# S4 convolution kernel: the low powers with their amplitude by exponentials and a product in PSUM, the first block's seeds ahead of its steps, its gate on the result

## The chip, the cores and the metric

The program runs on one core of a Trainium2 chip. Its time is the device time of one execution in microseconds (us), lower is better. The engines of the core are PE (TensorE: matmuls, with PEld for the loading of weights), DVE (VectorE), ACT (ScalarE), POOL (GpSimd) and SP (SyncE, which here issues most transfers). Each has an instruction queue of its own that runs in order, and they wait for each other by semaphores. SBUF and PSUM are the memories on the chip; PSUM takes the results of PE.

## The reference, cut to what matters

All arrays are float32; B = 1, L = S = 2048, D = 640, N = 192, F = 1536.

```python
def _A_ref(u, A_re, A_im, B_re, B_im, C_re, C_im, log_dt, Dskip):
    dt = jnp.exp(log_dt)[:, None]
    logdA = dt * (A_re + 1j * A_im)
    dB = dt * (B_re + 1j * B_im)
    l = jnp.arange(L)
    P = jnp.exp(logdA[:, :, None] * l[None, None, :])
    K = jnp.einsum("dn,dnl,dn->dl", C_re + 1j * C_im, P, dB).real
    # y = causal convolution of u with K along L, by FFTs of length 2 L
    ...
    return y + u * Dskip[None, None, :]

def _B_ref(x, w_gate, w_up, w_down):
    return ((x @ w_gate) * (x @ w_up)) @ w_down

x = A_u
sa, ca, ga, sb, cb, gb = the six rows of (_silu(c) @ w_mod)
h = _layernorm(x) * (1 + ca) + sa
x = x + ga * _A_ref(h, ...)
h = _layernorm(x) * (1 + cb) + sb
return x + gb * _B_ref(h, w_gate, w_up, w_down)
```

For one channel and one state, with rho and theta the real and imaginary parts of dt A, and amp and psi the size and the angle of C dB, the kernel K needs amp exp(rho l) cos(theta l + psi) for 2048 values of l, summed over the 192 states.

## The kernel before

**Tiling.** The 640 channels are taken in NB = 5 blocks of 128 (P). A block's 192 states are taken in 2 halves of 96, and a half in 4 steps of 24, so there are 40 steps (NK) of 24 states and 10 halves. The 2048 values of l are split into a low part (powers 0 to 7, times 64 for one of two tables) and a high part, so that a long table is an outer product of two short ones.

**The seeds of a block** (u_seeds) are made in segments, SEG0 for block 0 in the startup and SEG for the others in the loop, each letter a small step. s_l loads; s_a to s_c turn A, B and C into rho, theta and the product of B and C in a PSUM tile with the states transposed. s_d(h) makes the integer angles of half h by shifts (DL and DH, the low and the high ones). s_r(h) makes the multiples of rho: RL (1, 2 and 4 times rho) and RH (11 multiples for the high parts). s_e takes exponentials on ACT: seven powers of exp(64 rho) into LP, RH in place, RL in place. s_f, s_G, s_g and s_h give amp and the arctangent of the angle, transposed into PSUM; s_v copies amp into RL's fourth row and turns the angle into the integer psi. For block 0, s_e of the second half is put off (LATE, due at 15000).

**The tables** are POOL's. tab_ph(hf) makes LH, the low angles of half hf, with psi added in `weighted`. tab_eq(hf) makes LQ, amp times exp(rho l) for l = 0 to 7: one copy, one product and two doublings from RL. For each step n, `outer` (L817) writes three tables: Ph (LH plus DH, integer angles), EP (LP times RH) and EQ (LQ times RH). EP, EQ and the angle tables have two buffers each, LQ and LH one.

**A step** has four parts: ACT turns angles into sine and cosine by trig() (an Abs, a sine, and a cosine as the sine of pi/2 less the Abs) into PSUM tiles tra and trb, used in turn; DVE multiplies them with EQ and EP into QtA, PtA, PtB and QtB (L872, L878, L898); PE sums products over states into the PSUM tile kg (L913, L928). In trig(), where the source tile may be overwritten (the PtA parts), the Abs is taken in place of it; otherwise it goes to an SBUF tile `ab`.

**Around the steps** run, piece by piece, the FFT stages on PE (u_pre reads the normalized input h back, u_g, u_c and u_d go to the spectrum and back), the modulation rows from w_mod (L458), the statistics of the layer norm (u_stats: BN_STATS and BN_AGGR, L568) and the writing of x2d. In u_pre the four pieces of block 0 are multiplied by the gate row, on POOL (L966); for the other blocks the gate is in dt2 and dcol already. In u_d the result of the convolution in PSUM is added to the input, xs (L1110).

**What sets the order.** Table SCHED gives each piece a due time: a number of thousands for a half step of the loop, with 2t and 2t+1 for pass t of `for t in range(3 * NK + 24)`, and negative thousands for the startup, whose segments are SEG0's. Pieces are written out in the order of their due times; each engine then takes its own in that order. SP's queue holds the loads in that order too: a load into a buffer in use stands there until the buffer is free, and what is behind it stands as well. After the loop, from about 536 us on, comes the tail: the second layer norm and the GLU, in matmuls.

`act` (L320) is the helper through which every operation of ACT goes.

Of the kernel before, what the change touches and what calls it, by code (L numbers as in the profile page):

```python
# [10 lines left out]
F32 = mybir.dt.float32  # L11
# [21 lines left out]
    mr=(((-87997, 8001), (-87996, 11000)), ((-87999, 2000), (-88997, 8000)), ((-88999, -86998), (-89000, -87998))),  # L33
    st=(
        (-88993, 5000),
        (-101000, -92000),
# [4 lines left out]
        (-94000, -87995),  # L41
        (-98000, -87994),
        (1000, 20000),
        (1, 19000),
        (-91998, -87000),
        (-88995, 6000),
        (-87993, 13000),
        (-99000, -91000),
        (-88994, 16001),
        (-98998, -86999),  # L50
# [22 lines left out]
    e0=(15000,),  # L73
# [101 lines left out]
    low=(  # L175
        (14000, 40001, 64000, 88000, 111001, 139000, 163000, 187000, 209000),
        (18000, 42001, 68001, 92001, 113000, 139001, 163001, 185002, 209002),
    ),
# [136 lines left out]
def tile_kernel(ctx: ExitStack, tc: tile.TileContext, I, out):  # L315
# [20 lines left out]
    mults = const.tile([P, 14], F32, name="mults")  # L336
    for k, m in enumerate((1536, 1024, 512, 0, 8, 16, 24, 32, 40, 48, 56, 1, 2, 4)):
        V.memset(mults[:, k : k + 1], float(m))
# [60 lines left out]
    shr = kconst.tile([P, D], F32, name="shr")  # L399
    t_tw = kconst.tile([P, 32, 2, 64], F32, name="t_tw")  # L400
# [70 lines left out]
    def u_fold():  # L471
# [17 lines left out]
        V.tensor_tensor(sh[:, 0:1], sh[:, 0:1], gg[:, 0:1], op=OP.mult)  # L489
# [12 lines left out]
        act(xa[:, 4, 0:P], pt[:, P : 2 * P])  # L502
# [83 lines left out]
    LQ = pk1.tile([P, 96, 8], F32, name="LQ")  # L586
# [4 lines left out]
    RL = pk1.tile([P, 2, 4, 96], F32, name="RL")  # L591
    DH = [pk1.tile([P, 4, 192], I32, name=f"DH{i}") for i in range(3)]
    DL = [pk1.tile([P, 4, 192], I32, name=f"DL{i}") for i in range(2)]
    for d_ in DH:
        V.memset(d_[:, 0], 0)

    def u_seeds(db):
# [5 lines left out]
        prm = pk1.tile([P, 2, N], F32, name="prm")  # L603
        cr, ci = tb_[:, 2, :], tb_[:, 3, :]
        rho, f, amp = prm[:, 0, :], prm[:, 1, :], prm[:, 0, :]
        x, u, y, v = tb_[:, 0, :], tb_[:, 1, :], ta[:, 1, :], ta[:, 1, :]
# [24 lines left out]
        def free(h, *kinds):  # L631

            hf = 2 * db + h
            for k_ in kinds:
                if k_ in ("ph", "ep", "eq") and hf >= 3:
                    need(1, k_, 4 * (hf - 3) + 3)
                elif k_ in ("lh", "lq") and hf >= 2:
                    need(1, k_, hf - 2)
# [15 lines left out]
        def s_b():  # L654
            pb = bank("pb")
            act(pb, tb_[:, 0:2, :])
            V.tensor_tensor(ta, pb, cr.unsqueeze(1).to_broadcast([P, 2, N]), op=OP.mult)
            V.tensor_tensor(pb, pb, ci.unsqueeze(1).to_broadcast([P, 2, N]), op=OP.mult)
            V.tensor_tensor(x, ta[:, 0, :], pb[:, 1], op=OP.subtract)
            V.tensor_tensor(y, ta[:, 1, :], pb[:, 0], op=OP.add)  # L660
# [9 lines left out]

        def s_d(h):
            ps, q = T["ps"], T["q"]
            sti = q[:, 1].bitcast(I32).rearrange("p (s r) -> p s r", r=24)
            free(h, "lh", "ph")
            if h == 0:
                V.tensor_copy(sti, ps[:, 1])
# [6 lines left out]
            if h:  # L683
                V.tensor_tensor(t64, sti, shl[:, 5:6].unsqueeze(2).to_broadcast([P, 8, 24]), op=OP.logical_shift_left)
            mark("step", 2 * db + h)

        def s_r(h):
            ps = T["ps"]
            free(h, "ep", "eq", "lq")
            V.tensor_tensor(g4(Rl[h])[:, 0:3], ps[:, 0, hs[h]].unsqueeze(1).to_broadcast([P, 3, 4, 24]),  # L690
                            mults[:, 11:14].unsqueeze(2).unsqueeze(3).to_broadcast([P, 3, 4, 24]), op=OP.mult)
            V.tensor_tensor(g4(Rh[h]), ps[:, 0, hs[h]].unsqueeze(1).to_broadcast([P, 11, 4, 24]),
                            mults[:, 0:11].unsqueeze(2).unsqueeze(3).to_broadcast([P, 11, 4, 24]), op=OP.mult)
# [10 lines left out]
        def s_e(*hh):  # L704
            lp, rh, rl = (halves(R, hh) for R in (LP, RH, RL))
            for l in range(1, 8):
                act(lp[:, :, :, l], rl[:, :, 0], AF.Exp, scale=64.0 * l)
            act(rh, rh, AF.Exp)
            act(rl[:, :, 0:3], rl[:, :, 0:3], AF.Exp)
            for h in hh:  # L710
                mark("lp", 2 * db + h)

        def s_f():
# [3 lines left out]
            V.scalar_tensor_tensor(amp, u, dt2[:, db : db + 1], pe[:, 1], op0=OP.mult, op1=OP.mult)  # L717
            V.scalar_tensor_tensor(pe[:, 0], pe[:, 0], 1e-37, u, op0=OP.max, op1=OP.add)
            V.reciprocal(pe[:, 0], pe[:, 0])
# [4 lines left out]
        def s_G():  # L724
            if db:
                ps = bank("ps2")
            else:
                ps = ring(ps_tr, [P, 2, 512], "tr")[:, :, :N]
            T["ps2"] = ps.rearrange("p c (s r) -> p c s r", r=24)
            trans(amp, T["ps2"][:, 0])  # L730
            if db == 0:
                for h in range(2):
                    act(g4(Rl[h])[:, 3], T["ps2"][:, 0, hs[h]])
# [9 lines left out]
        def s_v():  # L743
            ps = T["ps2"]
            if db:
                for h in range(2):
                    V.tensor_copy(g4(Rl[h])[:, 3], ps[:, 0, hs[h]])
            V.tensor_scalar(psi, ps[:, 1], 4294967296.0 / math.pi, 536870912.0, op0=OP.mult, op1=OP.add)

            def weighted(h):  # L750
# [1027 lines left out]
```

## Time and profile before

| | us |
|---|---|
| runs of the kernel before | 990.01, 992.87, 998.23 |
| their median | 992.87 |
| the profiled execution | 990.33 |
| its span in the trace | 988.6 |
| PE busy | 887.3 (90%) |
| DVE busy | 760.7 (77%) |
| ACT busy | 579.9 (59%) |
| POOL busy | 577.4 (58%) |

The span is from the first to the last instruction of the trace; 1.7 us of the execution lie around it. The granted clock of TensorE was 0.958 of full speed over the span. "Busy" is the time in which an engine ran an instruction that does work. A row of a timeline gives the start, the duration of one instruction, the engine, the line, the operation and out<-in; in square brackets stands how long the engine had been idle before and what ended it. Rows of a chain of waits give the start, the time that the chain spends there, the engine and what it did. Rows of sums of waits read: engine, output and line, what it waited for, us in total, times, longest. The page's lines as they bear on the change stand in the prediction.

### The profile page before, as it was taken

What the parts mean: (1) busy time and instruction counts of PE and PEld (TensorE: products, weight loads), DVE (VectorE), ACT (ScalarE), POOL (GpSimd) and SP (SyncE); (2) the same over time, 40 slices, a digit from 0 to 9 for tenths busy, and PEclk for the clock granted to TensorE, in tenths of its full rate; (3) what the DMA queues carried; (4) which work ended last, traced back from release to release, by engine and by line L of the source; (5) the groups of instructions that cost most, each with busy time, mean ns of one, the idle gap of its engine ahead of it and who ended that gap; (6) DMA issues with size and microseconds to landing.
All of it is one profiled execution on the core that took longest, in us unless ns stands there. A gap on an engine that the chain in (4) does not pass through costs nothing.

```text
span 988.6 us, 26668 instructions
## 1 busy us (share of the span) xinstructions
PE 887.3 (90%) x11190; PEld 726.3 (73%) x11190; DVE 760.7 (77%) x1311; ACT 579.9 (59%) x1019; POOL 577.4 (58%) x424
## 2 busy tenths in 40 slices
PE   4854898999798699989988999999999999999998
PEld 3643656676575477677666888889998888889998
DVE  8798479887988977896899877787585977677452
ACT  5769999977888797974664322235464332224330
POOL 4987899799779989960145667641022454451000
PEclk9976899999989989999999999999999999999999
DMA  7665666443545553558733453445536222212241
GB/s 243 240 172 196 224 211 205 142 138 120 142 151 142 172 155 106 183 187 281 217 102 106 134 186 104 137 159 168 198 134 216 85 80 80 81 54 77 83 161 54
DMA packets 141961, 148.96 MB, mean 151 GB/s; under 512 B 8976, under 2 KB 120080, under 8 KB 140432
## 3 DMA queue, kind: packets, MB, share of 16 engines
q1 hardware_dynamic: 140688, 146.33, 46.9%
q8 instruction: 88, 1.44, 0.6%
q10 hardware_dynamic: 1152, 0.92, 0.3%
q14 instruction: 33, 0.27, 0.1%
HBM read 108.36 MB, written 38.86 MB: 149 GB/s over the span
## 4 chain that ended last, share of the span: by engine, by line
PE 58%; DVE 14%; ACT 13%; issue 6%; POOL 5%; DMA 2%; SPq 0%; DVEq 0%; ACTq 0%; POOLq 0%
PE pa L1196 26%; PE pa L1611 16%; ACT tra L320 2%; ACT trb L320 2%; PE psfb L995 2%; DVE QtA L872 2%; PE psfc L995 2%; PE psfb L1055 1%; PE kg L928 1%; POOL EQ L817 1%; PE psfa L1055 1%; PE kg L913 1%; PE psfc L1055 1%; PE psfb L950 1%; PE psfa L995 1%
## 5 line engine op out<-in xcount | busy, mean ns | idle before, releaser
L817 POOL TENSOR_TENSOR EQ<-LQ,RH 128x1536 f32<-128x1536 f32 x40 | 124.2, 3105 | 15.1 <-DVE QtB L872 14.9
L320 ACT ACTIVATE z<-pa 128x512 f32<-128x512 f32 x24 | 14.4, 599 | 167.1 <-PE pa L1196 120.5
L1160 DVE TENSOR_TENSOR wsgl<-wga,wsgh 128x640 fp32r<-128x640 f32 x72 | 68.1, 948 | 46.8 <-ACT wsgh L320 46.6
L320 ACT ACTIVATE wsgh<-wga 128x640 fp32r<-128x640 f32 x72 | 52.6, 732 | 72.0 <-PE pa L1611 48.6
L1560 POOL TENSOR_TENSOR z<-z,s 128x512 f32<-128x512 f32 x24 | 33.5, 1394 | 98.6 <-DVE s L1559 98.6
L1611 PE MATMUL pa<-wsgh,sh 128*128 128x384 f32 (+1 forms) x304 | 69.6, 310 | 0.0
L1611 PE MATMUL pa<-wsgh,sl 128*128 128x384 f32 (+1 forms) x304 | 69.2, 308 | 0.0
L1611 PE MATMUL pa<-wsgl,sh 128*128 128x384 f32 (+1 forms) x304 | 69.1, 309 | 0.0
L1172 POOL TENSOR_TENSOR tf<-wur,wgb 128x256 f32<-128x256 f32 x24 | 19.2, 801 | 80.7 <-DVE wtl L1160 54.7
L817 POOL TENSOR_TENSOR EP<-LP,RH 128x768 f32<-128x768 f32 x40 | 66.1, 1652 | 0.0
L817 POOL TENSOR_TENSOR Phb<-LH,DH 128x1536 int32<-128x1536 int32 x20 | 62.3, 3113 | 2.2 <-ACT tra L320 2.1
L817 POOL TENSOR_TENSOR Pha<-LH,DH 128x1536 int32<-128x1536 int32 (+1 forms) x21 | 62.4, 2972 | 1.8 <-ACT trb L320 1.4
L872 DVE TENSOR_TENSOR QtA<-tra,EQ 128x1024 f32<-128x1024 f32 x40 | 47.0, 1216 | 17.0 <-ACT tra L320 8.5
L1160 DVE TENSOR_TENSOR wtl<-tf,wth 128x256 fp32r<-128x256 f32 (+1 forms) x72 | 59.9, 858 | 0.0
L872 DVE TENSOR_TENSOR QtA<-trb,EQ 128x1024 f32<-128x1024 f32 x40 | 47.0, 1215 | 12.2 <-ACT trb L320 7.0
L928 PE MATMUL kg<-QtB,PtB 64*32 64x64 f32 x2560 | 47.0, 225 | 8.1 <-DVE QtB L872 8.0
L928 PEld LDWEIGHTS kg<-QtB,PtB 64*32 64x32 f32 x2560 | 40.3, 112 | 15.5 <-DVE QtB L872 9.0
L1558 DVE TENSOR_TENSOR s<-pa,s 128x512 f32<-128x512 f32 x24 | 16.6, 690 | 45.2 <-PE pa L1196 40.1
L1196 PE MATMUL pa<-sl,wth 128*128 128x512 f32 x144 | 45.2, 395 | 2.1 <-DVE sl L1160 2.1
L1611 PEld LDWEIGHTS pa<-wsgh,sl 128*128 128x128 f32 x304 | 46.6, 188 | 0.0
L1611 PEld LDWEIGHTS pa<-wsgh,sh 128*128 128x128 f32 x304 | 46.5, 188 | 0.0
L1611 PEld LDWEIGHTS pa<-wsgl,sh 128*128 128x128 f32 x304 | 46.5, 188 | 0.0
(602 smaller groups left out, 2926.9 us busy)
## 6 DMA issues: line engine op xcount, KB each, us to landing
wga<-wdg SPq DMA_DIRECT2D x24, 640.0 KB, 3.9
wga<-B_w_gate SPq DMA_DIRECT2D x12, 640.0 KB, 6.1
wgb<-B_w_gate SPq DMA_DIRECT2D x24, 320.0 KB, 3.4
wur<-B_w_up SPq DMA_DIRECT2D x24, 320.0 KB, 3.9
xb<-x2d SPq DMA_DIRECT2D x6, 1280.0 KB, 6.8
TVb<-WD SPq DMA_DIRECT2D x22, 256.0 KB, 3.4
t_tw<-w_mod SPq DMA_DIRECT2D x3, 1600.0 KB, 7.4
t_ti<-w_mod SPq DMA_DIRECT2D x3, 1600.0 KB, 7.5
```

Of the source, the lines that this page charges most:

```text
L320: return S.activation(o, i, f, **kw)
L817: G.tensor_tensor(o.rearrange("p x (h l) -> p x h l", l=8), lo.unsqueeze(2).to_broadcast([P, rows, nh, 8]), hi.rearrange("p h x -> p x h") ...
L872: return [lambda h=h: V.tensor_tensor(Qt[:, :, :, 32 * h : 32 * h + 32], tr[:, ::-1] if h else tr[:, :, :, ::-1], e[:, :, 32 * h : 32 * h ...
L928: PE.matmul(kg[j * 32 : j * 32 + 32, dd, :], PtB[lo : lo + 64, c, r, :], QtB[lo : lo + 64, c, r, :], start=False, stop=dd == 7 and c == 1, ...
L995: PE.matmul(r[c][par * 64 : par * 64 + 64, i, :], t_tw[:, k0 + k, c, :], src[:, k, :], start=True, stop=True, tile_position=(0, par * 64))
L1055: PE.matmul(r[par][:, i], w, v, start=c == 0, stop=c == 1, tile_position=(lo, 0))
L1160: V.tensor_tensor(lo, v, hi, op=OP.subtract)
L1172: G.tensor_tensor(t[:, 0:2], u[:, 0:2], g[:, 0:2], op=OP.subtract)
L1196: PE.matmul(ps, w[a][:, k], x[b][:, l], start=n == 0 and m == 0, stop=n == 2 and m == len(ks) - 1)
L1558: V.tensor_tensor(S67[i], ps, S6[i], op=OP.add)
L1560: G.tensor_tensor(ZT[i], ZT[i], S67[i], op=OP.add)
L1611: PE.matmul(ACC[tb][t][c], x[:, ts], w[:, cs], start=st, stop=f == NF - 1 and n == 2 and (c == 0 or t % 2 == 1))
```

## The change

It has six parts.

1. **Low powers.** tab_eq is gone from POOL. LQ has three halves as buffers. ACT takes exp(rho l) for l = 1 to 7 into LQ in s_e, as it does for LP, in place of the exponentials of RL; s_q copies amp from its PSUM tile to LQ's power 0 and multiplies the seven others by amp out of PSUM, on DVE. RL keeps only rho, so s_r copies 96 values a half in place of the product of 288.
2. **PSI.** In `weighted`, POOL did two operations for each of the two halves. Now `plus` adds psi over all states of the block and `minus` is done for each half (four operations for block 0, three for the others).
3. **The first block's seeds.** SEG0 is put in another order: both halves' exponentials, LQ products and shifts are in the startup, LATE is gone, and EP of step 1 and EQ of step 0 are made earlier on POOL. In table `st` the second numbers of the block's statistics move behind those pieces; two modulation rows (`mr`) have their second parts in the loop.
4. **The gate.** u_pre no longer multiplies by the gate row on POOL; u_d of block 0 multiplies the result in PSUM by the row (tile ggr) on DVE ahead of adding it to xs. The row of shifts `sh` is no longer multiplied by it.
5. **trig().** Where the Abs went to `ab`, it goes into the PSUM tile in which the cosine then replaces it.
6. **Tiles.** DH is one tile for all, prm is gone, and the temporary ones of the seeds share places.

The diff, cut to its core:

```diff
-    mr=(..., ((-88999, -86998), (-89000, -87998))),
+    mr=(..., ((-88999, 1100), (-89000, 100))),
     st=(
...
-        (-101000, -92000),
+        (-101000, -87500),
...
-        (-94000, -87995),
-        (-98000, -87994),
+        (-94000, -85900),
+        (-98000, -85800),
...
-    e0=(15000,),
...
-SEG0 = ("l", "a", "b", "c", "ud", "r", "x", "e", "f", "G", "g", "D", "h", "v", "R", "")
-SEG = ("l", "a", "b", "c", "ud", "D", "r", "R", "x", "E", "f", "g", "h", "v")
-P_PH, P_EP, P_MOD = 3, 6, 1
+SEG0 = ("l", "a", "b", "c", "iud", "r", "x", "e", "f", "Gg", "q", "R", "hv", "DX", "", "Q", "")
+SEG = ("l", "a", "b", "c", "iud", "D", "r", "R", "x", "E", "f", "g", "h", "v")
+P_PH, P_EP, P_EQ, P_PSI, P_MOD = 3, 6, 9, 12, 1
...
-    LQ = pk1.tile([P, 96, 8], F32, name="LQ")
+    LQ = pk1.tile([P, 3, 96, 8], F32, name="LQ")
...
-            V.tensor_tensor(g4(Rl[h])[:, 0:3], ps[:, 0, hs[h]].unsqueeze(1).to_broadcast([P, 3, 4, 24]),
-                            mults[:, 11:14].unsqueeze(2).unsqueeze(3).to_broadcast([P, 3, 4, 24]), op=OP.mult)
+            V.tensor_copy(Rl[h].rearrange("p (s r) -> p s r", r=24), rho_)
...
             for l in range(1, 8):
-                act(lp[:, :, :, l], rl[:, :, 0], AF.Exp, scale=64.0 * l)
+                act(lp[:, :, :, l], rl, AF.Exp, scale=64.0 * l)
             act(rh, rh, AF.Exp)
-            act(rl[:, :, 0:3], rl[:, :, 0:3], AF.Exp)
+            for l in range(1, 8):
+                act(lq[:, :, :, l], rl, AF.Exp, scale=float(l))
...
+        def s_q(*hh):
+            lq, a = halves(LQ, hh), T["amp"][:, hh[0] : hh[-1] + 1]
+            V.tensor_copy(lq[:, :, :, 0], a)
+            V.tensor_tensor(lq[:, :, :, 1:8], lq[:, :, :, 1:8], a.unsqueeze(3).to_broadcast([P, len(hh), 96, 7]), op=OP.mult)
...
+            def plus(w):
+                G.tensor_tensor(t64[:, w], t64[:, w], psi[:, w], op=OP.add)
+
+            def minus(h):
+                G.tensor_tensor(g5(Dl[h])[:, 0, :, 0, :], t64[:, hs[h]], g5(Dl[h])[:, 0, :, 1, :], op=OP.subtract)
...
-    def tab_eq(hf):
...
-        G.tensor_copy(LQ[:, :, 0:1], rl[:, 3].unsqueeze(2))
-        G.tensor_tensor(LQ[:, :, 1:2], rl[:, 3].unsqueeze(2), rl[:, 0].unsqueeze(2), op=OP.mult)
-        double(LQ, (rl[:, 1], rl[:, 2]), OP.mult)
...
         if ab is None:
-            ab = pk.tile([P, 512], F32, name="ab", bufs=1)
-            av = ab
+            ab = av = cv
...
-        if db == 0:
-            G.tensor_tensor(h, h, xa[:, 4, 0:P].unsqueeze(1).to_broadcast([P, 4, P]), op=OP.mult)
...
+        if db == 0:
+            V.tensor_tensor(ps, ps, ggr.unsqueeze(1).to_broadcast([P, 4, P]), op=OP.mult)
         V.tensor_tensor(xs, ps, xs, op=OP.add)
```

On the engines this stands as follows. The first place is DVE in the startup, from the last small step of the angle (ptb or pta from psfb) on; st and mv are the statistics, and f16a and gha are tiles of the input rows that they read. Before:

```order
L722 TENSOR_SCALAR pta<-psfb 128x192
L568 BN_STATS st_282<-f16a 128x6 x2
L569 BN_AGGR mv_95<-st_282 128x2
L568 BN_STATS st_290<-gha 128x6 x2
L569 BN_AGGR mv_95<-st_290 128x2
L677 CAST DL_159<-psfc 128x4x24
L680 TENSOR_TENSOR DL_159<-psfa,shl 128x12x24
L680 TENSOR_TENSOR DH_156<-psfa,shl 128x8x24
L680 TENSOR_TENSOR DL_159<-psfa,shl 128x12x24
L680 TENSOR_TENSOR DH_156<-psfa,shl 128x8x24
L684 TENSOR_TENSOR ptb<-psfa,shl 128x192
L748 TENSOR_SCALAR ptb<-tra 128x192
```

After:

```order
L712 COPY LQ<-tra 128x96
L713 TENSOR_TENSOR LQ<-LQ,tra 128x96x7
L687 COPY RL<-psfc 128x96
L688 TENSOR_TENSOR RH<-psfc,mults 128x1056
L745 TENSOR_SCALAR ptb<-tra 128x192
L675 TENSOR_TENSOR ptb<-psfa,shl 128x192
L676 CAST DL_155<-psfc 128x4x24
L679 TENSOR_TENSOR DL_155<-psfa,shl 128x12x24
L679 TENSOR_TENSOR DH<-psfa,shl 128x8x24
L679 TENSOR_TENSOR DL_155<-psfa,shl 128x12x24
L679 TENSOR_TENSOR DH<-psfa,shl 128x8x24
L564 BN_STATS st_371<-f16a 128x6 x2
```

The first statistics now stand behind the LQ product of the first half, RL and RH of the second and all its shifts; the rows between them and QtA of step 0 are statistics and, once more, an LQ copy and product. SP's order of loads is the same in both kernels.

The second place is ACT between the trig of step 1 and that of step 2, in the loop's first passes. Before:

```order
L320 ACTIVATE tra<-PtAa,halfpi 128x512
L320 ACT_TABLE_LOAD
L320 ACTIVATE LP<-RL 128x96 x7
L320 ACTIVATE RH<-RH 128x1056
L320 ACTIVATE RL<-RL 128x288
L320 ACTIVATE prm<-pta,dt 128x192
L320 ACTIVATE Kta<-kg 128x512
L320 ACTIVATE ab<-Pha 128x512
L320 ACT_TABLE_LOAD
L320 ACTIVATE trb<-Pha 128x512
```

After:

```order
L316 ACTIVATE tra<-PtAa,halfpi 128x512
L316 ACTIVATE pta<-pta,dt 128x192
L316 ACTIVATE Kta<-kg 128x512
L316 ACTIVATE trb<-Pha 128x512 x2
L316 ACTIVATE trb<-trb,halfpi 128x512
```

The exponentials of block 0's second half and both table loads are gone from here, and the Abs (the first of the two rows in trb<-Pha) writes the ring's tile.

The third place is DVE in block 2, around the seeds' last step, s_v; RL, LQ and ptb belong to the seeds and QtA, PtAa and QtB to the steps. Before:

```order
L872 TENSOR_TENSOR QtB<-tra,EQ_146 128x16x32 x2
L872 TENSOR_TENSOR QtA<-trb,EQ_145 128x32x32 x2
L747 COPY RL<-psfc 128x96 x2
L748 TENSOR_SCALAR ptb<-psfc 128x192
L878 TENSOR_TENSOR PtAa<-tra,EP_147 128x1024
```

After:

```order
L862 TENSOR_TENSOR QtB<-tra,EQ_144 128x16x32 x2
L862 TENSOR_TENSOR QtA<-trb,EQ_143 128x32x32 x2
L712 COPY LQ<-psfc 128x192
L713 TENSOR_TENSOR LQ<-LQ,psfc 128x192x7
L745 TENSOR_SCALAR ptb<-psfc 128x192
L868 TENSOR_TENSOR PtAa<-tra,EP_145 128x1024
```

The copy of amp and its product with seven powers stand where two small copies stood, ahead of psi (ptb<-psfc).

More of the change, by code (lines that the diff above doesn't have):

```diff
@@ L335, in tile_kernel @@
     V.memset(halfpi, math.pi / 2)
[L336 to L337 removed]
+    mults = const.tile([P, 11], F32, name="mults")
+    for k, m in enumerate((1536, 1024, 512, 0, 8, 16, 24, 32, 40, 48, 56)):
         V.memset(mults[:, k : k + 1], float(m))
```

128 lines of the change are left out of this document (57 added, 71 removed).

## The prediction

> **What bounds the kernel now.** I read the page first, then a table of busy time by stretch, the sums of waits, the chain of waits, and the startup in order of time. From the page, the chain that ended last, by engine:
>
> ```profile
> PE 58%; DVE 14%; ACT 13%; issue 6%; POOL 5%; DMA 2%; SPq 0%; DVEq 0%; ACTq 0%; POOLq 0%
> ```
>
> Busy time of each engine in stretches of the span (length, then PE, PEld, DVE, ACT, POOL):
>
> ```profile
> core 0: us, PE busy (x) PEld busy (x) DVE busy (x) ACT busy (x) POOL busy (x), PEclk, DMA share, GB/s
> ...
> 376.00:426.00 50.00, 46.77 (x1112) 35.66 (x1114) 40.15 (x51) 41.60 (x72) 49.61 (x27) 0.97 0.44 134
> ...
> 536.00:988.00 452.00, 445.18 (x2372) 394.70 (x2372) 312.72 (x504) 157.38 (x304) 164.59 (x151) 1.00 0.38 125
> ```
>
> The tail from 536 us on is PE alone (445.18 of 452.00 us) and the change puts nothing there, so all is decided in the first half. There four engines are each 80 to 99% busy. POOL is the fullest by far, 49.61 of 50.00 us late in the loop, and yet it is on only 5% of the chain. The sums of waits between 26 and 490 us say why:
>
> ```profile
> POOL EQ L817 <- DVE QtB L872: 14.9, 5, 5.0
> ...
> ACT PtAa L320 <- POOL Pha L817: 3.8, 4, 2.5
> ...
> DVE QtA L872 <- POOL EQ L817: 2.8, 2, 1.8
> ...
> DVE QtA L872 <- POOL LH L799: 2.7, 2, 1.4
> ...
> DVE PtAa L878 <- POOL LH L799: 2.4, 1, 2.4
> ```
>
> POOL works ahead into double buffers until a buffer is not free (14.9 us of waiting for QtB to release EQ); the others wait for it in four rows that sum to 11.7 us, with only crumbs below them. A POOL with less to do will mostly wait longer for EQ's release. What sets the pace is the loop DVE, ACT, PE, in which the chain changes engine every few us. By the chain, DVE holds 14% of 988.6 us, 138 us, and as the tail is PE's, nearly all of that lies in the first 490 us: about 0.3 of it.
>
> **Startup: SEG0, the late exponentials, the row statistics.** The first step's QtA (30.57) follows on DVE behind the last BN_STATS, and these are paced by their loads. DVE in order of time, then SP's issues of the loads, and a PE row that waits for one of them:
>
> ```profile
> 16.92 0.87 DVE L568 BATCH_NORM_STATS2 st<-f16a 128x6 f32<-128x320 f32 x2
> ...
> 19.11 0.20 DVE L677 CAST DL<-psfc 128x96 int32<-128x96 f32 x1
> ...
> 20.49 0.34 DVE L684 TENSOR_TENSOR ptb<-psfa,shl 128x192 int32<-128x192 int32 x1
> ...
> 21.92 0.89 DVE L568 BATCH_NORM_STATS2 st<-gha 128x6 f32<-128x320 f32 x2 [0.82 <-DMA gha<-A_u]
> ...
> 24.45 1.25 DVE L692 TENSOR_TENSOR RH<-psfc,mults 128x1056 f32<-128x1056 f32 x1
> 27.19 0.89 DVE L568 BATCH_NORM_STATS2 st<-gha 128x6 f32<-128x320 f32 x2 [1.50 <-DMA gha<-A_u]
> ...
> 30.57 2.31 DVE L872 TENSOR_TENSOR QtA<-trb,EQ 128x1024 f32<-128x1024 f32 x2
> 34.35 0.69 DVE L898 TENSOR_TENSOR PtB<-trb,EP 128x512 f32<-128x512 f32 x1 [0.34 <-ACT trb L320]
> ```
>
> ```profile
> 18.98 0.33 SPq L560 DMA_DIRECT2D gha<-A_u  x1
> 19.36 0.43 SPq L451 DMA_DIRECT2D t_ti<-w_mod  x1
> 22.83 0.33 SPq L560 DMA_DIRECT2D gha<-A_u  x1
> ...
> 26.45 2.40 PE L458 MATMUL psfb<-t_ti,sil 128*128 128x256 f32 x10 [0.96 <-DMA t_ti<-w_mod]
> ```
>
> SP's queue is in order and the change leaves its order as it is. The reload of gha stands in it until the statistics of the old gha are done (18.98), and behind it t_ti and the next gha. In the new order DVE does, ahead of the first BN_STATS, the first LQ copy and product, RL and RH of the second half, psi, the 64-fold shift and the second half's five shifts. Sizes: the product is 672 elements with one operand in PSUM; from PtB (512 elements, 0.69) and QtA (two of 1024 in 2.31, some 1.2 for one) that is about 0.69 + 160 x 1.0 ns = 0.85. RH takes 1.25, the cast and shifts 1.4 (19.11 to 20.49), the copies about 0.25 each, psi and the 64-fold shift 0.34 each: 4.6 us in all, as some overlap, against the old order, which took part of this in the gaps of 0.82 and 1.50 us before the later gha. So gha's reload goes from 18.98 to about 23.6, t_ti to 24.0, and the third gha's statistics from 27.19 to about 31.9. QtA of step 0 then starts near 35.3, 4.7 late; PE's t_ti matmuls and the ACT copy behind them are late by the same.
>
> On the other side, the second half's exponentials leave the loop:
>
> ```profile
> 46.74 1.28 ACT L320 ACT_TABLE_LOAD   x1
> 48.04 1.43 ACT L320 ACTIVATE LP<-RL 128x96 f32<-128x96 f32 x7
> ...
> 53.90 0.46 ACT L320 ACTIVATE prm<-pta,dt 128x192 f32<-128x192 f32 x1 [3.22 <-DMA pta<-A_A_re]
> ...
> 55.38 1.28 ACT L320 ACT_TABLE_LOAD   x1
> ```
>
> They run from 46.74 to 50.68 (53.90 less the 3.22 of idling), 3.9 us, and with the second load 5.2 of ACT. But ACT idles 3.22 us just behind them until pta lands, so about 2.0 of it was felt at most, and DVE, late by 4.7 at step 0, is by then what the others wait for. I let a third of the lateness be taken up in short waits along steps 1 to 3 (ACT for the trig ring, an idle gap of DVE ahead of step 3). That leaves **+3.1 us**. Ends: +4.7 if nothing is taken up, and -5.2 if all of the removed ACT time had been on the path. I stay near the upper end, because the rows of DVE and DMA are late in the order itself.
>
> By the Trainium skill ("ScalarE: Activation LUTs", "What ACT_TABLE_LOAD costs") a change of function set costs 1.28 us for the load and 1.38 for a drain. This trace shows the 1.28 and LP starting 0.02 us behind the load, with no drain after it; the net one load that goes would by the page free 2.66 us of ACT, and by the row 1.28, in either case where ACT waits for pta.
>
> **The low powers.** POOL loses, for each half, a copy, a product and two doublings; ACT gains seven exponentials into LQ and loses one into RL:
>
> ```profile
> L777 POOL TENSOR_TENSOR LQ<-LQ,RL x20: 555/720/885, 18.0 to 403.3; 128x192 f32<-128x192 f32 x10, 128x384 f32<-128x384 f32 x10
> L811 POOL COPY LQ<-RL x10: 348/360/375, 17.3 to 402.0; 128x96 f32<-128x96 f32 x10
> L812 POOL TENSOR_TENSOR LQ<-RL x10: 391/396/402, 17.5 to 402.2; 128x96 f32<-128x96 f32 x10
> ```
>
> ```profile
> 94.33 2.63 ACT L320 ACTIVATE LP<-RL 128x192 f32<-128x192 f32 x7
> 96.76 1.97 ACT L320 ACTIVATE RH<-RH 128x2112 f32<-128x2112 f32 x1
> 98.62 0.67 ACT L320 ACTIVATE RL<-RL 128x576 f32<-128x576 f32 x1
> ```
>
> POOL: 0.36 + 0.40 + 2 x 0.72 = 2.2 us a half, 22 us over ten halves. ACT: the seven new exponentials have the shape of LP's, 2.63, minus 0.67 of RL: +1.96 for each of blocks 1 to 4, 7.8 in all. The chain of waits has ACT's exponentials of block 1 and block 4 in it, and not those of blocks 2 and 3; its rows (start, us), with one of POOL for block 2:
>
> ```profile
> 94.33 2.63 ACT LP L320 x7
> ...
> 189.03 0.36 POOL ptb L752
> ...
> 345.30 2.68 ACT LP L320 x7
> ```
>
> So 2.0 and 2.0 count in full. For block 2 the chain runs over POOL's first sum with psi (189.03), which psi, later by the exponentials ahead of it and by the product before it on DVE, can hold up; POOL has a lead there, so I take 0.7 of 2.0. For block 3, the arctangent, and behind it a transposition that stands in PE's queue, come 2.0 later, and PE has idle time ahead of it: less than half, 0.8. Together **+5.5** (ends 4.0 and 7.8).
>
> DVE's side: LQ copy and product, 1344 elements, 1.2 + 320 x 1.0 ns = 1.5 plus about 0.45 for the copy. What goes, and POOL's gate on the first block:
>
> ```profile
> L690 DVE TENSOR_TENSOR RL<-psfa,mults x6: 444/444/445, 85.2 to 344.8; 128x288 f32<-128x288 f32 x6
> L747 DVE COPY RL<-psfa x4: 247/252/258, 102.3 to 277.8; 128x96 f32<-128x96 f32 x4
> ...
> L966 POOL TENSOR_TENSOR hfc<-hfc,f16a x2: 1282/1297/1312, 123.6 to 140.3; 128x512 f32<-128x512 f32 x2
> ```
>
> RL becomes a copy of a third of the size (0.25 for 0.44, twice a block) and the two old copies go (0.25 each): net 1.5 + 0.45 - 0.4 - 0.5 = 1.05 a block, 4.2 in four. **The gate** goes from POOL (4 x 1.28 = 5.1 us) to DVE as four products of 512 elements with one operand in PSUM, 0.69 each: 2.8. DVE's 7.0 us count by its share of the chain in the first half, 0.3: **+2.1** (ends 0, if all fall in DVE's waits for trig, and 7.0).
>
> **The Abs in PSUM.** In the steps that had a separate tile ab, Abs could run before DVE gave the trig ring's buffer back; now it waits with the sines. Where the chain goes from QtA to ACT's sine, as here (start, us, from the chain of waits), the sine stood directly behind the release with its Abs done:
>
> ```profile
> 296.13 0.52 ACT ab L320
> ...
> 331.60 1.22 DVE QtA L872
> ...
> 332.84 0.61 ACT trb L320
> ```
>
> An Abs holds ACT for 0.52 us (296.13), and three such places (257, 333, 379 us) are on the chain: up to 1.6; the cosine may read PSUM a little faster, so half, **+0.8** (ends -0.5 and 1.6).
>
> **PSI and POOL's relief.** One sum over both halves and two differences for four operations of 0.39 save POOL 0.2 a block. Of the 11.7 us of waits for POOL I credit **-1.0**: POOL is on the chain at 21 to 60 and 184 to 198 us only, and in the second place behind QtB's release and psi, which the change makes no earlier. Ends 0 and -11.7.
>
> **Sum.** 3.1 + 5.5 + 2.1 + 0.8 - 1.0 = +10.5 on the profiled execution's 990.33 (span 988.6 and 1.7 around it): about 1000.8. The median of the runs, 992.87, lies 2.5 above the profiled one; as the runs shown spread from 990.01 to 998.23, I take the sum as it is, **1000 us**, rounded down as waits elsewhere take up some.
>
> **Rivals.**
> 1. *POOL was the pace-maker* (ends on the other side). If the waits for Pha, EQ and LH are what delays each half, the 27 us taken from POOL, most of it where POOL is 49.61 of 50.00 busy, remove all four rows, 11.7, and ACT's and DVE's additions fall into their own waits: 990.3 - 11.7 = 978.6. It decides from the point where EQ and Ph have no lead over DVE. For it: the fullest engine. Against: 14.9 us in which POOL waits for DVE, and 5% of the chain.
> 2. *The lateness at the start is taken up*, since the exponentials gone from 46.7 to 56.7 free ACT for the steps there, and the exponentials of blocks 2 and 3 stay hidden: only 4.0 of the exponentials and part of DVE's 2.1 remain, minus 1.0: 990.3 + 4 = about 994. This is also how it looks if putting seeds ahead of the steps does what its name says and no more.
> 3. *Everything adds*: 4.7 + 7.8 + 7.0 + 1.6 - 1.0 = +20, 1010 us. For it: ACT and DVE at 80% or more through the loop; against: their waits of several us for each other.
>
> **How the numbers follow.** The forecast gets 0.42, rival 1 0.14, rival 2 0.27, rival 3 0.17. A measurement of this kernel tells about 1% from no change, 983 to 1003 us around 992.87. Faster takes most of rival 1: 0.12. Slower takes rival 3 and the upper part of the forecast: 0.36. The rest, 0.52, is within 1%. With a tenth left out at each end the range is 984 to 1008; the forecast's own is 996 to 1005.
>
> **What would show it.** QtA of step 0 at about 35 us, and SP's second gha reload at 23 to 24: the startup step; at 30 or below it falls. ACT's seven exponentials into LQ near 2.6 us and on the chain in blocks 1 and 4. POOL's wait for QtB well above 14.9 us with the distance from step to step unchanged: relief wasted; a shorter period would prove rival 1. Abs directly behind QtA's end on the chain: the PSUM step. The tail must keep its 452 us from end of loop to end. The forecast is wrong if the loop, measured from QtA of step 0 to that of step 39, becomes shorter.

## The result

| | median us | runs | ratio to before (95% interval) |
|---|---|---|---|
| before | 995.20 | 4, 990.01 to 998.23 | |
| after | 1023.83 | 4, 1021.59 to 1028.10 | 1.0298 (1.0238 to 1.0358) |

The change makes the kernel 3.0% slower, about 30 us. Predicted were 1000 us, 10.5 us more than before, and at most 1008: the direction was right, the size was not. (The profile that was taken of the changed kernel has a chain of waits only for the tail, so the loop is read here from the other views.)

### The profile after

The same stretches as before (length, then PE, PEld, DVE, ACT, POOL); the last one is the tail, which now begins 34 us later:

```profile
core 0: us, PE busy (x) PEld busy (x) DVE busy (x) ACT busy (x) POOL busy (x), PEclk, DMA share, GB/s
26.00:76.00 50.00, 35.19 (x494) 28.15 (x493) 38.00 (x68) 22.30 (x38) 34.32 (x19) 0.76 0.61 214
...
376.00:426.00 50.00, 41.95 (x946) 33.18 (x946) 35.38 (x48) 39.95 (x68) 38.30 (x21) 0.92 0.41 124
...
570.00:1022.00 452.00, 445.24 (x2372) 394.86 (x2372) 313.43 (x504) 157.23 (x304) 164.40 (x151) 1.00 0.39 125
```

The tail keeps its 452 us. In the loop every engine is less busy than it was: POOL 38.30 of 50 us where it was 49.61, but DVE also 35.38 for 40.15. The same 50 us hold other steps in the two kernels, so here is the whole loop too: from QtA of step 0 to QtA of step 39 it takes 437 us for 407, and DVE is busy for 349 us of them (339 before), PE 348 (339), ACT 355 (351), POOL 340 (369). The work has not become too much for one engine; the engines wait more for each other. The sums of waits of the changed kernel between 30 and 525 us (engine, output, line, what it waited for, us, times, longest), and those of the kernel before for two of them:

```profile
POOL EQ L806 <- DVE QtB L862: 27.0, 10, 7.0
...
POOL Pha L806 <- ACT trb L316: 21.9, 7, 7.6
...
DVE PtB L888 <- ACT trb L316: 14.4, 11, 3.1
...
ACT TVb L316 <- PE psfc L455: 10.0, 1, 10.0
ACT trb L316 <- DVE QtA L862: 9.6, 6, 4.4
```

```profile
DVE PtB L898 <- ACT trb L320: 9.3, 12, 1.8
...
ACT trb L320 <- DVE QtA L872: 2.5, 1, 2.5
```

POOL's relief went into waiting, as predicted: 27.0 us for QtB where it was 14.9, and 21.9 for trig to release Ph (1.4 before). DVE and ACT now wait longer for each other in both directions, 14.4 for 9.3 and 9.6 for 2.5 in the rows shown. Over all rows of QtA, PtA and PtB, DVE waits 45 us for ACT where it was 31, and ACT waits 26 us for DVE to release the trig tiles where it was 12.

Where the time is lost along the program is seen from the start of QtA in some of the 40 steps (us, from DVE's rows), with the lateness against before. Blocks 1 to 4 get their seeds in about the steps 5 to 9, 13 to 16, 21 to 25 and 29 to 36:

| step | before | after | late | lost since the row above |
|---|---|---|---|---|
| 0 | 30.57 | 35.25 | 4.7 | 4.7 |
| 1 | 39.32 | 45.68 | 6.4 | 1.7 |
| 2 | 49.74 | 62.51 | 12.8 | 6.4 |
| 3 | 60.76 | 72.37 | 11.6 | -1.2 |
| 5 | 86.73 | 98.04 | 11.3 | -0.3 |
| 9 | 132.41 | 149.49 | 17.1 | 5.8 |
| 13 | 167.64 | 184.19 | 16.6 | -0.5 |
| 16 | 203.73 | 224.66 | 20.9 | 4.4 |
| 21 | 257.21 | 278.81 | 21.6 | 0.7 |
| 25 | 302.51 | 329.09 | 26.6 | 5.0 |
| 29 | 338.20 | 365.66 | 27.5 | 0.9 |
| 36 | 411.38 | 445.82 | 34.4 | 7.0 |
| 39 | 437.69 | 472.38 | 34.7 | 0.3 |

A good 11 us are lost by step 5, and then 4 to 7 in each block's seeds; between them nearly nothing.

### The startup, row by row

DVE, SP, PE and ACT of the changed kernel in order of time (start, duration, idle time before in brackets):

```profile
21.15 0.88 DVE L564 BATCH_NORM_STATS2 st<-f16a 128x6 f32<-128x320 f32 x2
...
35.25 2.31 DVE L862 TENSOR_TENSOR QtA<-trb,EQ 128x1024 f32<-128x1024 f32 x2
```

```profile
23.21 0.33 SPq L556 DMA_DIRECT2D gha<-A_u  x1
23.59 0.43 SPq L448 DMA_DIRECT2D t_ti<-w_mod  x1
```

```profile
30.79 4.60 PE L455 MATMUL psfb<-t_ti,sil 128*128 128x256 f32 x10 [4.35 <-DMA t_ti<-w_mod]
35.18 3.92 PE L455 MATMUL psfc<-t_ti,sil 128*128 128x384 f32 x10
```

```profile
39.14 0.48 ACT L316 ACTIVATE TVb<-psfc 1x384 f32<-1x384 f32 x1 [10.04 <-PE psfc L455]
39.52 1.21 ACT L316 ACTIVATE trb<-Pha 128x512 f32<-128x512 int32 x2
```

So far it went as worked out: gha's reload at 23.21 (23.6 was predicted), t_ti at 23.59, QtA of step 0 at 35.25 (35.3). What follows was not seen. The copy of the modulation row (TVb) stands in ACT's queue ahead of the third trig of step 0 (the last row) and waits 10.04 us for PE; it runs 7.0 us later than before (at 32.11). Of these, 4.3 come from t_ti's landing. The other 2.7 come from PE: the first ten matmuls take 4.60 us where they took 2.40, at a granted clock of 0.50 in these rows against 1.00 before, and the next ten 3.92 where they took 3.39. So step 1 is 6.4 us late, where the prediction let the 4.7 of step 0 shrink. And then the modulation column, ten operations on 128x5 elements and less ahead of QtA of step 2 (eleven before), takes 6.86 us (55.65 to 62.51) where it took 2.52. Three of its rows after, with POOL's of the same time, and two of the same rows before:

```profile
56.44 1.44 DVE L481 TENSOR_SCALAR mcol<-mcol 128x5 f32<-128x5 f32 x1
57.91 3.01 DVE L482 TENSOR_TENSOR mcol<-mcol 128x5 f32<-128x5 f32 x1
...
61.44 1.07 DVE L486 TENSOR_TENSOR dt<-dt,mcol 128x4 f32<-128x4 f32 x1
```

```profile
55.23 2.61 POOL L776 TENSOR_TENSOR LH<-LH,DL 128x384 int32<-128x384 int32 x2
57.80 3.08 POOL L806 TENSOR_TENSOR EQ<-LQ,RH 128x1536 f32<-128x1536 f32 x1
60.85 1.64 POOL L806 TENSOR_TENSOR EP<-LP,RH 128x768 f32<-128x768 f32 x1
```

```profile
48.22 0.17 DVE L484 TENSOR_SCALAR mcol<-mcol 128x5 f32<-128x5 f32 x1
48.43 0.24 DVE L485 TENSOR_TENSOR mcol<-mcol 128x5 f32<-128x5 f32 x1
```

The three slow operations end at 57.88, 60.92 and 62.51, and POOL's operations end at 57.84, 60.88 and 62.49. An operation of 0.17 us stood until a POOL operation was over. Before, POOL was at a row of operations of 0.4 to 0.6 us at that time, so the same wait was short.

### A block's seeds

ACT and DVE of the changed kernel in block 1:

```profile
106.00 2.63 ACT L316 ACTIVATE LP<-RL 128x192 f32<-128x192 f32 x7
108.43 1.96 ACT L316 ACTIVATE RH<-RH 128x2112 f32<-128x2112 f32 x1
110.30 2.62 ACT L316 ACTIVATE LQ<-RL 128x192 f32<-128x192 f32 x7
```

```profile
115.90 0.53 DVE L712 COPY LQ<-psfa 128x192 f32<-128x192 f32 x1 [5.73 <-PE psfa L625]
116.25 1.56 DVE L713 TENSOR_TENSOR LQ<-LQ,psfa 128x1344 f32<-128x1344 f32 x1
...
119.87 2.35 DVE L862 TENSOR_TENSOR QtA<-trb,EQ 128x1024 f32<-128x1024 f32 x2 [1.80 <-ACT trb L316]
```

The same place on DVE before:

```profile
102.27 0.42 DVE L747 COPY RL<-psfa 128x96 f32<-128x96 f32 x2 [3.78 <-PE psfa L629]
...
106.25 2.35 DVE L872 TENSOR_TENSOR QtA<-trb,EQ 128x1024 f32<-128x1024 f32 x2 [3.29 <-ACT trb L320]
```

The new exponentials take 2.62 us and the product 1.56, as estimated. Copy and product stand in DVE's queue behind the arctangent's transposition, and DVE idles 5.73 us there, 1.95 longer than before, as ACT takes the arctangent behind the exponentials. Behind the product QtA of step 6 still waits 1.80 us for ACT's sine and cosine, which stand behind the arctangent in their turn. So in this block the added exponentials on ACT make the step late, and the product fits into a wait that was there already (3.29 us before).

### The profile page after: what moved, and what is told of

Read it like the earlier page. It is cut to its first block, busy times and chain, and to the rows that moved or that the text cites. A ratio compares the mean times of both kernels' runs of the same rounds, so it can differ in the third digit from the quotient of the medians.

```text
span 1022.5 us, 26655 instructions
## 1 busy us (share of the span) xinstructions
PE 895.2 (88%) x11190; PEld 733.0 (72%) x11190; DVE 773.8 (76%) x1314; ACT 589.8 (58%) x1052; POOL 552.2 (54%) x376
## 3 DMA queue, kind: packets, MB, share of 16 engines
q8 instruction: 88, 1.44, 0.6%
## 5 line engine op out<-in xcount | busy, mean ns | idle before, releaser
L316 ACT ACTIVATE z<-pa 128x512 f32<-128x512 f32 x24 | 14.4, 599 | 167.3 <-PE pa L1186 115.8
L806 POOL TENSOR_TENSOR Pha<-LH,DH 128x1536 int32<-128x1536 int32 (+1 forms) x21 | 62.4, 2972 | 22.7 <-ACT trb L316 21.9
L862 DVE TENSOR_TENSOR QtA<-trb,EQ 128x1024 f32<-128x1024 f32 x40 | 47.0, 1217 | 16.1 <-ACT trb L316 7.2
L1548 DVE TENSOR_TENSOR s<-pa,s 128x512 f32<-128x512 f32 x24 | 16.6, 691 | 45.2 <-PE pa L1186 40.1
```

Source lines behind the costliest of these rows:

```text
L316: return S.activation(o, i, f, **kw)
L806: G.tensor_tensor(o.rearrange("p x (h l) -> p x h l", l=8), lo.unsqueeze(2).to_broadcast([P, rows, nh, 8]), hi.rearrange("p h x -> p x h") ...
L862: return [lambda h=h: V.tensor_tensor(Qt[:, :, :, 32 * h : 32 * h + 32], tr[:, ::-1] if h else tr[:, :, :, ::-1], e[:, :, 32 * h : 32 * h ...
L1548: V.tensor_tensor(S67[i], ps, S6[i], op=OP.add)
```

## The experiments

The theories are these. A: the Abs in PSUM costs some half a us in most steps. B: the startup's lateness is carried to the end. C: the low powers on ACT and DVE are the loss. D: several parts cost, and hide each other. L: the modulation column waits for POOL. Times are medians; each ratio is to the kernel before, run on the same chip. The rows come from four chips, on which the kernel before had medians of 992.3 us (e1 to e4), 992.0 (e6 to e9), 996.5 (e10 to e12) and 994.2 (e13), so the ratios compare better than the times.

| run | what differs | us | ratio (95% interval) |
|---|---|---|---|
| e1 | after, Abs in SBUF | 1021.29 | 1.0276 (1.0234 to 1.0318) |
| e2 | before, Abs in PSUM | 1003.10 | 1.0074 (1.0037 to 1.0111) |
| e3 | after, statistics early | 1020.19 | 1.0260 (1.0217 to 1.0304) |
| e4 | after, column's temporaries in PSUM | 1021.13 | 1.0265 (1.0221 to 1.0309) |
| e6 | after, low powers on POOL, one LQ buffer | 1009.36 | 1.0169 (1.0111 to 1.0228) |
| e7 | after, gate on POOL | 1025.13 | 1.0317 (1.0243 to 1.0390) |
| e8 | before, five more exponentials a block | 1000.53 | 1.0105 (1.0031 to 1.0180) |
| e9 | after, without the product by amp | 1020.95 | 1.0294 (1.0232 to 1.0355) |
| e10 | e1 + e3 + e4 | 1007.75 | 1.0105 (1.0065 to 1.0146) |
| e11 | e10 + e6 | 995.26 | 0.9984 (0.9968 to 1.0001) |
| e12 | e11, Abs in PSUM | 1001.81 | 1.0066 (1.0040 to 1.0091) |
| e13 | e10, without the product by amp | 1002.27 | 1.0079 (1.0050 to 1.0109) |

**The Abs out of PSUM (e1).**

```diff
-            ab = av = cv
+            ab = av = cv if at_ is None else at_.rearrange("p r m -> p (r m)")
...
-        tr = trig(PH[n].rearrange("p (a r) m -> p a (r m)", a=2)[:, :, 512:768])
+        if n + 1 < NK:
+            OUT[n + 1] = dict(PA=ring(pk, [P, 2, 16, 32], "PtA"))
+        tr = trig(PH[n].rearrange("p (a r) m -> p a (r m)", a=2)[:, :, 512:768], None, OUT[n + 1]["PA"][:, 1] if n + 1 < NK else None)
```

> The changed kernel, but the Abs of the third part of a step goes to SBUF again (into the half of PtA that the next step will use, since the old tile no longer fits), so that it need not wait for the trig ring. Theory A (an Abs behind the ring's release costs about 0.5 us in most of the 40 steps, not in three): 10 to 15 us of the 29 come back, the waits of DVE's PtB for trb fall from 14.4 towards 9 us, total 1009 to 1014. Rival B (the startup's lateness, 11.6 us at step 3, is carried to the end and the Abs costs next to nothing): at most 2 us come back. Rival C (the exponentials and products of the low powers do it): at most 2 us.

2.5 us came back (1023.8 to 1021.3), near what theories B and C expected and not A's 10 to 15. The waits of PtB for trb did fall as A has it, from 14.4 to 10.5 us, but the total hardly followed. The interval overlaps that of the changed kernel, and so do those of e3 and e4 below: none of the three is told from no gain by itself.

**The Abs alone, in the kernel before (e2).**

```diff
...
-            ab = pk.tile([P, 512], F32, name="ab", bufs=1)
-            av = ab
+            ab = av = cv
...
```

> The kernel before, with only the Abs moved into the PSUM tile. Theory A: 10 to 15 us slower than before, 1003 to 1008. Rivals B and C: within 2 us of before; my prediction's own term was +0.8.

It is slower by 7 us by the ratio and by 11 by the median of ten runs that spread from 996 to 1010: more than rivals B and C and the prediction's +0.8 allow; theory A's 10 to 15 fit the median and not the ratio. So the same edit costs 7 or more in one kernel and gives 2.5 back in the other. In the profiled run of e2, the slowest of the ten, the modulation column was slow, too (50.70 to 58.09, with rows of 1.44 and 3.01 us): 7.2 of the 17.3 us by which it is late at step 39 are there at step 5. So a part of its price is that of theory L.

**The statistics early (e3).**

```diff
-        (-101000, -87500),
+        (-101000, -92000),
...
-        (-94000, -85900),
-        (-98000, -85800),
+        (-94000, -87995),
+        (-98000, -87994),
...
-        (-91998, -85700),
+        (-91998, -87000),
...
-        (-99000, -87400),
+        (-99000, -91000),
...
-        (-98998, -85600),
+        (-98998, -86999),
```

> The changed kernel, but with the due times that block 0's statistics had before, so that they stand ahead of most of the second half's seeds on DVE; nothing else moves. All theories expect gha's reload near 20.3 instead of 23.2 us and QtA of step 0 near 32 instead of 35.3. Theory A: only part of the 11.6 us at step 3 comes back, 3 to 5 us in the total. Rival B: 8 us or more come back, about 1015 or less. Rival C: 0 to 2.

QtA of step 0 starts at 31.73 us and that of step 3 at 62.76, only 2.0 late instead of 11.6. But at step 39 it is 28.6 late, and the total is 3.6 us less than the changed kernel's, as theory A expected and not the 8 or more of rival B. Of 9.6 us won at the start, 6.1 are left at the end of the loop in the profiled run: the lateness of the start is carried on in part only.

**The modulation column (e4).**

```diff
-        g1, sg, rg, sh, gg = (mcol[:, i, :] for i in range(5))
+        h1, sg, rg, sh, gg = (mcol[:, i, :] for i in range(5))
+        g1, gp = (pc[:, 64 + 8 * i : 64 + 8 * i + NB] for i in range(2))
...
-        V.tensor_tensor(g1, g1, sg, op=OP.mult)
-        V.reciprocal(rg, g1)
+        V.tensor_tensor(h1, g1, sg, op=OP.mult)
+        V.reciprocal(rg, h1)
...
-        V.tensor_tensor(gg, p3[:, 2], g1, op=OP.mult)
+        V.tensor_tensor(gg, p3[:, 2], h1, op=OP.mult)
+        V.tensor_tensor(gp, p3[:, 2], h1, op=OP.mult)
```

(and gp in place of gg in the two products after it)

> The changed kernel, but three of the five-column temporaries of the modulation column are kept in the PSUM tile, so that no DVE operation there has two SBUF inputs, at the price of one more operation. Theory L (the 6.9 us from mcol's first operation to QtA of step 2, against 2.5 before, are waits of DVE for a POOL operation to end): the stretch falls to about 3 us, QtA of step 2 starts near 58.5 instead of 62.5, and up to 4 us come back in the total. Rival (the operations were slow for another reason, or PSUM makes no difference): the stretch stays at 6 to 7 us and the total does not move.

DVE of e4, the operations that had been slow and QtA of step 2:

```profile
56.42 0.17 DVE L482 TENSOR_SCALAR psfb<-psfb 128x5 f32<-128x5 f32 x1
56.63 0.16 DVE L483 TENSOR_TENSOR mcol<-psfb,mcol 128x5 f32<-128x5 f32 x1
...
57.45 0.16 DVE L488 TENSOR_TENSOR dt<-dt,psfb 128x4 f32<-128x4 f32 x1
...
57.81 2.35 DVE L864 TENSOR_TENSOR QtA<-trb,EQ 128x1024 f32<-128x1024 f32 x2
```

POOL beside them:

```profile
55.41 2.59 POOL L778 TENSOR_TENSOR LH<-LH,DL 128x384 int32<-128x384 int32 x2
57.96 3.10 POOL L808 TENSOR_TENSOR EQ<-LQ,RH 128x1536 f32<-128x1536 f32 x1
```

All of them take 0.16 or 0.17 us, and all run beside POOL's sums into LH, the second of which had held one of them for 1.44 us; they are done before POOL's EQ starts at 57.96. The stretch falls from 6.86 to 2.0 us and step 2 starts 4.7 earlier. Theory L is shown. In the total 2.7 us came back, too little to be told from none.

**The low powers on POOL again (e6).**

```diff
-            for l in range(1, 8):
-                act(lq[:, :, :, l], rl, AF.Exp, scale=float(l))
+            act(rl[:, :, 0:3], rl[:, :, 0:3], AF.Exp)
...
-            V.tensor_copy(lq[:, :, :, 0], a)
-            V.tensor_tensor(lq[:, :, :, 1:8], lq[:, :, :, 1:8], a.unsqueeze(3).to_broadcast([P, len(hh), 96, 7]), op=OP.mult)
+            for h in hh:
+                V.tensor_copy(Rl[h][:, 3], T["amp"][:, h])
...
+    def tab_eq(hf):
...
+        G.tensor_copy(LQ[:, :, 0:1], rl[:, 3].unsqueeze(2))
+        G.tensor_tensor(LQ[:, :, 1:2], rl[:, 3].unsqueeze(2), rl[:, 0].unsqueeze(2), op=OP.mult)
+        double(LQ, (rl[:, 1], rl[:, 2]), OP.mult)
```

> The changed kernel with the low powers as before: RL of three multiples, its exponentials and amp's copy, LQ built by POOL in four operations a half; Abs, gate, startup and PSI stay changed. Theory C (the seven exponentials on ACT and the product on DVE, with what waits in order behind them, cost 4 to 6 us in each of blocks 1 to 4): 14 to 22 us of the 29 come back, total 1002 to 1010. Theory D (each part costs a little and they hide each other, so that undoing one alone gives back only 2 to 4): 3 to 5 us come back, about 1019.

14.5 us came back, theory C's lower end. Half of the loss is left. (This run also has a single LQ buffer again and POOL's old due times for it, as the kernel before has; they were not tried apart.)

**The gate (e7).**

```diff
+        if db == 0:
+            G.tensor_tensor(h, h, ggr.unsqueeze(1).to_broadcast([P, 4, P]), op=OP.mult)
...
-        if db == 0:
-            V.tensor_tensor(ps, ps, ggr.unsqueeze(1).to_broadcast([P, 4, P]), op=OP.mult)
```

> The changed kernel with the gate on POOL ahead of the first block's transform again. Theory C: at most 3 us come back (four products of 0.69). Theory D: 2 to 4.

Nothing came back (1025.1 for 1023.8, intervals that overlap): the gate on DVE has no price that these runs can show.

**More exponentials in the kernel before (e8).**

```diff
+            if db:
+                for l in range(1, 6):
+                    act(lp[:, :, :, l], rl[:, :, 0], AF.Exp, scale=64.0 * l)
             act(rh, rh, AF.Exp)
```

> The kernel before, with five of the seven exponentials into LP done twice in blocks 1 to 4: 1.88 us more of ACT a block at the very place where the change adds 1.96. Theory C: 6 to 12 us slower than before. If ACT's additions are hidden: within 2 us.

It is 8.5 us slower, ratio 1.0105. In block 1 the exponentials into LP take 4.37 us for 2.63, 1.74 more where 1.88 had been estimated, so about 7 us in four blocks: ACT's additions are on the path at about their full size. They are not so in each block. In the profiled runs the lateness against before grows by 3.3 us in steps 5 to 9, by 0.3 in 13 to 16, by 2.7 in 21 to 25 and by 3.3 in 29 to 36: in block 2 they stayed nearly hidden.

**Without the product (e9).**

```diff
-            V.tensor_tensor(lq[:, :, :, 1:8], lq[:, :, :, 1:8], a.unsqueeze(3).to_broadcast([P, len(hh), 96, 7]), op=OP.mult)
+            if db == 0:
+                V.tensor_tensor(lq[:, :, :, 1:8], lq[:, :, :, 1:8], a.unsqueeze(3).to_broadcast([P, len(hh), 96, 7]), op=OP.mult)
```

> The changed kernel without the product by amp in blocks 1 to 4 (left out, so the powers 1 to 7 lack amp): 1.56 us less of DVE a block, 6.2 in all. Theory C with the product as a part of the cost: 5 to 8 us come back. If only ACT's exponentials matter: at most 3.

2.9 us less, which the intervals do not tell from none. In the profiled runs it wins back 3.2 us in steps 13 to 16 and 2.0 in steps 29 to 36, and nothing in steps 5 to 9 and 21 to 25, so where the product has a price in these runs it is in blocks 2 and 4.

**Three undone (e10), and four (e11).** The edits are those above, together.

> The changed kernel with three things undone at once: Abs out of PSUM (as in e1), statistics early (e3), the modulation column's temporaries in PSUM (e4); the low powers stay on ACT and DVE. If the parts add, 2.5 + 3.6 + 2.7, less some 2 for what e3 and e4 both take away: about 7, total 1016 to 1018. If the parts hide each other (each alone meets another of them): 11 to 14 come back, total 1010 to 1012.

> As e10, and the low powers on POOL as well (e6). What stays of the change is the gate on the result, PSI and the second half's exponentials ahead of the steps. If the four parts are the whole loss: 990 to 996, level with before. If POOL's relief by gate and PSI and the exponentials gone from the first steps are worth something: 985 to 989. If the seeds ahead of the steps cost by themselves: 998 or more.

e10 won back 16.1 us, more than either expectation, where its three parts alone had won 2.5, 3.6 and 2.7. By the medians these parts hide each other (theory D): taking one of them away, the next wait stands in its place. That is not shown, though. In the spans of the profiled runs e1, e3 and e4 win 3.2, 5.9 and 2.7 us, together 11.8, and e10 wins 13.7, nearly the sum; and the intervals of the single gains are wide. e11 is level with the kernel before, at 0.9984: the four parts are the whole loss, and what is left of the change (gate on the result, PSI, the second half's seeds ahead of the steps) is worth nothing that can be measured, in either direction.

**From e11, the Abs alone (e12), and the product from e10 (e13).** The edits are the reverse of e1's and that of e9.

> As e11, but with the Abs in PSUM: the difference to e11 is the Abs alone in a kernel in which nothing else of the loss is left. By e2 (the Abs alone in the kernel before) it is 7 us; by e1 (out of the changed kernel) 2.5.

> As e10 (the low powers are all that is left of the loss, 10.5 us), without the product by amp in blocks 1 to 4 (left out, so the powers 1 to 7 lack amp). If the loss is ACT's exponentials alone (four times 1.96, and 8.5 in e8), at most 2 us come back: 1005 to 1008, ratio 1.008 or more. If the product counts as well with its full 1.56 in each block: 5 to 6 come back, ratio 1.004 to 1.006.

e12 is 6.5 us above e11 by the medians, 8 by the ratios (1.0066 less 0.9984), and the intervals lie apart. In its sums of waits the rows of the Abs have grown. e11, then e12:

```profile
DVE PtB L905 <- ACT trb L319: 11.9, 13, 3.0
...
ACT tra L319 <- DVE QtA L875: 4.7, 4, 1.9
...
DVE PtB L905 <- ACT tra L319: 4.3, 5, 2.5
...
ACT trb L319 <- DVE QtA L875: 3.3, 2, 2.7
```

```profile
DVE PtB L901 <- ACT trb L319: 14.5, 13, 2.1
...
ACT tra L319 <- DVE QtA L875: 10.3, 9, 4.7
...
DVE PtB L901 <- ACT tra L319: 6.4, 7, 2.4
...
ACT trb L319 <- DVE QtA L875: 5.9, 5, 3.5
```

ACT waits for QtA to release tra or trb fourteen times instead of six, and DVE's PtB then waits 20.9 us for the cosine instead of 16.2. The loss comes in some of the steps, not in all 40: in the profiled runs the distance from e11 to e12 is 1.8 us at step 5, 1.2 at step 21, 4.1 at step 29 and 6.7 at step 39. e13 is 0.26% below e10, 2.6 us, less than the product's 6.2 us of DVE; its 1.0079 lies at the edge of what was expected if the exponentials alone count. The two intervals overlap, so this is a size, not a proof.

**The account.** By ratios on about 993 us, with other parts undone: the low powers cost 1.21%, 12 us (e10 less e11), of which the product perhaps 2.6 and the exponentials with the copy of amp 9.4 (e13 less e11, 0.95%); the Abs 0.82%, 8 us (e12 less e11); startup and modulation column 1.03%, 10 us (e6 less e12, with the Abs in PSUM). Together 30 us, against the 29.6 of the change. This sum proves less than it seems. From e11 over e12 and e6 to the changed kernel one part is put back at a time, so the steps of that series must add up to the whole; what is tested is that its last step, the low powers with all the rest in place, has the same size (1.29%, 13 us) as with the rest undone. The 18 us of Abs and startup could fall to the two otherwise in another order. Each of the three rests on a difference of two ratios whose own intervals reach 2 to 6 us to each side; for the startup's two causes apart (the statistics and the column) the runs give only what each took back alone.

## Why the prediction was wrong

- **What bounds the loop.** Right. POOL's 27 us less of work bought nothing: its wait for QtB went from 14.9 to 27.0 us, and the rival by which POOL sets the pace fell. The credit of -1.0 was not there either (e11, with the gate and PSI as changed, is level).
- **Startup, +3.1.** The step to step 0 was right to 0.1 us. The sentence that failed is "I let a third of the lateness be taken up in short waits along steps 1 to 3". It grew instead, from 4.7 to 11.6 at step 3, by ACT's copy of a modulation row at the head of an in-order queue, and by DVE's column, whose operations now met long POOL operations; about 2 us of it are the Abs (9.6 late at step 3 in e1). The prediction had named that copy, as late "by the same", but put no price on the trig behind it, and the copy came 7.0 us late and not 4.7, as PE's granted clock was 0.50 for a part of its matmuls. About 10 us in the account: a term mis-sized by three, by mechanisms that the order and the rows of before could have suggested (the row behind which ACT stood idle for 1.02 us at 32.11 was there).
- **Low powers, +5.5, and DVE's share in +2.1.** The mechanism was right; the size was at or above the upper end that the text gave (7.8 for the exponentials): 9.4 us by e13 and e11, 8.5 for nearly the same work in e8. What failed is the cover granted to blocks 2 and 3. Block 3 had none (2.7 us in e8, 2.6 from e11 to e13). Block 2, put at 0.7, kept its cover in e8 (0.3) and not from e11 to e13 (1.9). Block 1, counted in full, showed 3.3 and 2.3, block 4 3.3 and 1.0; these are differences of single profiled runs.
- **The Abs, +0.8.** Mis-sized by eight to ten. I counted the three places at which the chain of waits of before went from QtA to a sine. In e12 ACT waits for QtA at fourteen places, eight more than in e11, and the cost is 6.5 to 8 us. That at these places another chain had stood only a little ahead, so that the added half us made this one the last, is how I read it; no run shows it place by place.
- **The gate, in +2.1.** No price (e7).
- **The range.** Its third rival, everything adds, was put at 1010 with 0.17 and its terms were the ends of the text; two of these ends (+4.7 for the startup and 1.6 for the Abs) were not ends, since they took the places on one chain for all places.

## What to carry to other kernels

In a loop in which three engines are 80% busy and wait for each other in turn, the chain of waits shows only one of several paths of nearly equal length: an operation of 0.52 us, put behind a wait in every step, cost 6.5 to 8 us here, between the 1.6 of the chain's three places and the 21 of all 40 steps. The places on the chain were the lower end of that price. When a kernel loses by many parts, undo them together and put one back: out of the changed kernel the Abs won back 2.5 us that could not be told from nothing, and put into a kernel free of the other losses it cost 6.5 to 8, clear of the noise. A row that is moved earlier on one engine makes late whatever stands in line behind the loads that it delays, and a copy for another purpose at the head of an in-order queue passes that on.

## What the runs showed of the hardware

**DVE stands behind a POOL operation.** A DVE operation of 0.17 us took 1.44, 3.01 and 1.07 us, ending 0.02 to 0.04 us after the POOL operation that ran beside it; with operands moved to PSUM (e4) it took 0.16 or 0.17. Two of the three had two SBUF inputs, the third one input and its output in SBUF. The Trainium skill ("SBUF — State Buffer", "SBUF: two separate sides") says that a pair of ports is shared by VectorE and GpSimd under an exclusive lock, held for a whole instruction, and that VectorE needs it with two SBUF inputs or in a mode with two ports. These rows agree, for two inputs by both measurements; that the operation with one input was in such a mode, no row shows. Not every operation with its input in SBUF was held: the reciprocal of the same column, which started at 60.95 beside POOL's EP (60.85 to 62.49), took 0.19 us.

**At a lower granted clock the same matmuls take longer.** In a step after block 1's seeds a group of 64 matmuls took 1.94 us in the changed kernel and 1.10 before, and a group of 16 took 1.98 and 1.09, the same work. The granted clock was 0.50 in these rows against 1.00 before (0.77 in 130 to 145 us against 1.00 in 115 to 130). After, then before:

```profile
135.91 1.94 PE L903 MATMUL kg<-QtA,PtAb 128*32 128x64 f32 x64
...
138.31 1.98 PE L940 MATMUL psfc<-ct,Kta 128*64 128x128 f32 x16
```

```profile
121.68 1.10 PE L913 MATMUL kg<-QtA,PtAb 128*32 128x64 f32 x64
...
123.03 1.09 PE L950 MATMUL psfc<-ct,Kta 128*64 128x128 f32 x16
```

ACT then waited 1.82 us for the second group, and from QtA of step 7 to that of step 9 another 3.4 us were lost. Up to QtA of step 39 the mean granted clock was 0.91 before and 0.89 after, and the same 7706 matmuls kept PE busy for 354.9 us before and 364.9 after. Whether the longer waits bring the clock down was not tried, nor how much of the 30 us goes this way; it is a part of each price above, not one beside them.
